# Turning q and k of two batches by a DMA transpose and ScalarE copies in a fused attention and feed-forward kernel

## The chip, the cores and the metric

The kernel runs on one core of a Trainium2 chip. A core has TensorE (PE), which multiplies matrices and can transpose a block by multiplying it with an identity, VectorE (DVE), ScalarE (ACT), GpSimd (POOL) and SyncE (SP), which here only issues transfers. Each engine takes its instructions in the order in which the program gives them to it, and waits on semaphores for what the others produce. Sixteen DMA engines move data; they are fed from queues on SP, ACT and POOL. SBUF is the on-chip memory of 128 partitions. PSUM, where TensorE writes its results, has eight banks, each of 512 fp32 values on every partition.

The metric is the device time in microseconds of one execution of the whole kernel.

## The reference

The inputs q, k and v have the shape (8 batches, 8 heads, 576 tokens, 64). All is fp32.

```
scores = (q @ k^T) / sqrt(64)
heads 0..3: key j is seen by query i if 0 <= i - j < 32          (local)
heads 4..7: key j is seen by query i if j <= i and j % 32 == i % 32   (strided)
x   = softmax(scores) @ v        -> tokens x 512   (4608 x 512, heads side by side)
h   = x @ w_in                   (512 -> 2048)
g   = max(h, 0) + alpha * min(h, 0)
out = g @ w_out                  (2048 -> 512)
```

## The kernel before

**Feed-forward.** The 4608 tokens are cut into nine stages of 512. A stage n has 32 steps. Steps 0 to 15 (`lin1_piece`, L571 to L596) each make one 128 x 512 block of h by four matmuls (L583); ScalarE makes the negative part (L591) and VectorE the result g (L594). Steps 16 to 31 make the output. In stage 1 they are `lin2_piece` (L600 to L628): four matmuls of 512 columns each (L622), and after every fourth step one output tile is copied by ScalarE (L627) and stored by SP (L628). From stage 2 on they are `lin2_fast` (L671 to L734), a scheme with fewer products that works with sums of blocks of g. Those sums (gsum, L652) are made by VectorE and GpSimd at fixed steps, and each pair of `lin2_fast` steps reads one of them.

**Attention.** A pair g is two heads of one batch, 4 pairs to a batch: pairs 4b and 4b + 1 are local, 4b + 2 and 4b + 3 strided. The work of batch n + 1 is done in small pieces between the steps of stage n. A list of pieces is built once (L475 to L545), and `attn_step` (L555) puts the next one out. For a counter g the pieces are in this order: scores of pair g (S, `score_both`), first product with v of pair g - 1 (P), the q transposes of pair g + 1's unit (T), a second P, the k transposes (Tk), and a third P for a strided pair. So batch 3's local q and k are turned while g is 11 and read by the scores of pairs 12 and 13; batch 4's while g is 15, read by those of pairs 16 and 17. These fall into stage 1's and stage 2's second halves. A batch's two local pairs share a pair of tiles, qTs[0] and kTs[0]; index e of them is the pair, and each pair's scores read one e.

**How local q and k get there.** For batches 0 to 4 a transfer (`load_qk`, L97) puts 9 consecutive tokens of the two heads of one pair on each partition, in fp32: partition 2p + e holds tokens 9p to 9p + 8 of pair e. A cast (`cast_l`, L177) makes an fp16 tile [128, 9, 2, 64]: partition, token t within the partition, head within the pair, feature. For batches 2 to 4 GpSimd does it in the list or ScalarE ahead of it. `transpose_piece` (L254) then transposes nine 128 x 128 blocks on TensorE (L269), five into one PSUM bank and four into another. For batch 2 and later ScalarE evicts both (L272 and L273, shown under the line of the helper, L207), and in doing so puts the tokens in order: token 9p + t comes from partition p of block t. Batches 5 to 7 take another way (`load_rows`, `turn_rows`): the load itself casts and lays the rows so that DMA transposes write qTs and kTs directly.

**Order and buffers around it.** `score_both` writes its scores into one two-bank PSUM tile (sp) and into two slots of a ring of three one-bank slots (ps); the products P, the transposes and two other users take slots from the same ring. The exponentials of the second half (L382) are not put out at once but by one per `attn_step` (the list `defer`). SP's queue has, in program order: the DMA transposes of finished attention outputs (`x_dma`, L446 and L443), those of strided q and k (`transpose_d`, L175), and the output stores. In the stretch before batch 3's turn, the casts of batch 3's q and k are in g = 9, pair 8's `x_dma` ends g = 9, and pair 9's comes late in g = 10.

Of the kernel before, what the change touches and what calls it, by code (L numbers as in the profile page):

```python
# [10 lines left out]
F16 = mybir.dt.float16  # L11
# [21 lines left out]
def kernel(  # L33
# [10 lines left out]
    nc = tc.nc  # L44
    keep = tc.keep_in_program_order
# [11 lines left out]
    hpool = ctx.enter_context(tc.tile_pool(name="half", bufs=4))  # L57
# [26 lines left out]
    DX = 2  # L84
    qTs = [cpool.tile([128, 2, 672], F16, name=f"qT{i}") for i in range(2)]
    kTs = [cpool.tile([128, 2, 672], F16, name=f"kT{i}") for i in range(2)]
# [8 lines left out]
    cast16 = {}  # L95
# [12 lines left out]
    NX = 5  # L108
# [13 lines left out]
    def turn_rows(b):  # L122

        for nm in "qk":
            t16 = loaded[(b, False, nm)]
            for e in range(2):
                o = qTs[0][:, e, 0:576] if nm == "q" else kTs[0][:, e, 32:608]
                keep(nc.sync.dma_start_transpose(
                    o.rearrange("r (w p) -> r w p", p=96), t16[0:96, 768 * e : 768 * e + 768]))

    def load_d(b):

        for nm, src in (("q", q), ("k", k)):
            keep(nc.gpsimd.dma_start(
                qks[nm][0:72], src[b, 4:8, :, :].rearrange("h (p t) d -> p h (t d)", t=8)))
# [41 lines left out]
    def cast_l(b, nm, eng="pool"):  # L177
        t16 = hpool.tile([128, 9, 2, 64], F16, tag=f"{nm}l16", bufs=2, name=f"{nm}l16")
        cast_copy(eng, t16, loaded[(b, False, nm)].rearrange("p f (t d) -> p t f d", t=9))
        cast16[(b, False, nm)] = t16  # L180

    def load_v(b, strided):


        if strided:
            st = spool.tile([128, 2048], F16, tag="v", bufs=2, name="stv")
            step = 2 if b == 0 else 4
            for h in range(0, 4, step):
                keep(nc.gpsimd.dma_start(
                    st[0:72, 512 * h : 512 * (h + step)].rearrange("p (h e) -> p h e", h=step),  # L190
                    v[b, 4 + h : 4 + h + step, :, :].rearrange("h (p t) d -> p h (t d)", t=8)))
            loaded[b] = st
        else:
            v16 = vls[b % 2]
            base = v[b, 0:1, 0:1, :]
            r0 = 32 if b < 2 else 0
            step = 12 if b == 0 else 24
            for c in range(0, 24, step):
                keep(nc.gpsimd.dma_start(
                    v16[r0:128, c : c + step, 0:64],  # L200
                    bass.AP(tensor=base.tensor, offset=base.offset + (96 * c - 32 + r0) * D,
                            ap=[[D, 128 - r0], [96 * D, step], [1, D]])))
            cast16[(b, False, "v")] = v16

    def cast_copy(eng, o, i):
        if eng == "act":
            keep(nc.scalar.copy(o, i))  # L207
        elif eng == "dve":
            keep(nc.vector.tensor_copy(o, i))
        else:  # L210
            keep(nc.gpsimd.tensor_copy(o, i))  # L211
# [42 lines left out]
    def transpose_piece(u, nm):  # L254

        b = u // 2  # L260
        early = b < NEARLY
        src = cast16[(b, False, nm)]
        dst = qTs[u % 2][:, :, 0:576] if nm == "q" else kTs[u % 2][:, :, 32:608]
        o = dst.rearrange("r e (p t) -> r e p t", t=9)
        tps = []
        for t0, t1 in ((0, 5), (5, 9)):
            tp = pspool.tile([128, 8, 64, 2], F16, tag="ps", name="tp")
            for t in range(t0, t1):
                keep(nc.tensor.transpose(  # L269
                    tp[:, t - t0].rearrange("r p e -> r (p e)"), src[:, t].rearrange("p f d -> p (f d)"), ident))  # L270
            tps.append(tp[:, 0 : t1 - t0].rearrange("r t p e -> r e p t"))
        cast_copy("act", o[:, :, :, 0:5], tps[0])  # L272
        cast_copy("dve" if early and (u or nm == "k") else "act", o[:, :, :, 5:9], tps[1])  # L273
# [186 lines left out]
    def feed(fn, g):  # L460
        pieces.append((g, fn))

    def T(u, nm):
        return lambda: transpose_piece(u, nm)

    def Sc(g, i):
# [2 lines left out]
    def Pv(g, i):  # L469
        return lambda: pv_piece(pairs[g], i)  # L470

    def X(g, eng=None):
        return lambda: x_piece(pairs[g], eng or ("act" if pairs[g].strided else "dve"))

    for g in range(7, npair + 2):  # L475
        c = g // 4
        a, p, t = g, g - 1, g + 1
        okA = 8 <= a < npair
        okP = 8 <= p < npair
        okT = 8 <= t < npair and t < 4 * NX and (t % 4 == 0 or t < 4 * DX and t % 2 == 0)  # L480
        nP = len(pairs[p].pgroups) if okP else 0
        seq = []
        if okA:
            seq.append(("S", lambda a=a: score_both(pairs[a])))
        if okP:
            seq.append(("P", Pv(p, 0)))
        if okT:
            seq.append(("T", T(t // 2, "q")))
        if 8 <= g - 2 < npair and not pairs[g - 2].xd:
            seq.append(("X", X(g - 2)))  # L490
        if okP:
            seq.append(("P", Pv(p, 1)))
        if okT:
            seq.append(("Tk", T(t // 2, "k")))
        if nP == 3:
            seq.append(("P", Pv(p, 2)))
        if not seq:
            seq.append(("N", lambda: None))

        todo = [(c, pr) for pr in range(2)] if g % 4 == 0 and 8 < g < npair else []  # L500

        if g % 4 == 1 and 9 <= g and c + 1 < B:
            todo = [(c + 1, nm) for nm in "qk"]
        lastP = max([i for i, z in enumerate(seq) if z[0] == "P"], default=len(seq) - 1)
        nslots = [i for i, z in enumerate(seq) if z[0][0] != "S"] or list(range(len(seq)))
        for i, (kind, fn) in enumerate(seq):
            extra = []
            if todo and i in nslots:
                left = len([z for z in nslots if z >= i])
                cnt = -(-len(todo) // max(1, left))  # L510
                extra = [todo.pop(0) for _ in range(min(cnt, len(todo)))]

            def run(fn=fn, extra=extra, g=g, c=c, kind=kind, lastp=(i == lastP), first=(i == 0),
                    second=(i == min(1, len(seq) - 1))):
                fn()
                for b, pr in extra:
                    if pr in ("q", "k"):
                        if b < NX:
                            cast_l(b, pr)
                        if b + 1 < NX:  # L520
                            load_qk(b + 1, pr)
                        continue
                    cast_v(b, pr, "pool")
                    if pr == 1 and b + 1 < B:
                        load_v(b + 1, True)
                if first and g % 4 == 2 and NX <= c + 1 < B:
                    turn_rows(c + 1)
                if lastp and g % 4 == 3 and NX <= c + 2 < B:
                    load_rows(c + 2, "k")
                if lastp:  # L530
                    if 4 * DX <= g - 1 < npair and pairs[g - 1].xd:
                        x_dma(pairs[g - 1])
                    if g % 4 == 3 and DX < c + 1 < B:
                        transpose_d()
                    if g % 4 == 2 and DX <= c and c + 1 < B:
                        load_d(c + 1)
                    if g % 4 == 1 and DX <= c and c + 1 < B:
                        load_v(c + 1, False)
                    if g % 4 == 1 and NX <= c + 2 < B:
                        load_rows(c + 2, "q")  # L540
                    if g == 8:
                        load_v(3, True)
                if second and 4 * DX <= g - 3 < npair and pairs[g - 3].xd and pairs[g - 3].strided:
                    after.append(lambda: x_copy(pairs[g - 3]))
            feed(run, g - 2 if kind == "X" else -1)  # L545

    pos = {"i": 0}
# [2 lines left out]

        return max(i for i, (g, _) in enumerate(pieces) if g == 4 * b + 3) + 1

    late, after = [], []

    def attn_step(end):  # L555
        while late:
            late.pop(0)()
        if pos["i"] < end:
            pieces[pos["i"]][1]()
            pos["i"] += 1  # L560
        if defer:
            defer.pop(0)()
        while after:
            after.pop(0)()

# [181 lines left out]
    def warm(n):  # L747

        for _ in range(n):
# [12 lines left out]
            name=nc.get_next_instruction_name(), act_func_set_id=6, ins=[], outs=[]  # L762
# [29 lines left out]
    def attn_n(n, end):  # L792
        for _ in range(n):
            attn_step(end)
        if n == 0:
            attn_step(0)
# [164 lines left out]
```

## Time and profile before

| | us |
|---|---|
| median of 3 runs | 301.82 (301.68 to 301.95) |
| the profiled execution's own time | 301.52 |
| its span | 299.7 |
| TensorE busy | 293.2 (98%) |
| VectorE busy | 219.1 (73%) |
| ScalarE busy | 178.6 (60%) |
| GpSimd busy | 171.9 (57%) |

All times in the profile are microseconds from the start of the span, unless they are marked ns. A line of a timeline gives the start, the duration, the engine, the line of the kernel, the operation, and what it writes and reads; xN is the number of instructions merged in it, and a bracket at the end is the engine's idle time before it, with what ended that. PE is a matmul, PEld a weight load, and SPq or POOLq the issuing of a transfer. A line of the chain that ended last gives the start, the duration, the engine, what it writes and its line. In groups of instructions the figures after the bar are the busy time in all, the mean of one in ns, and the engine's idle time before them. Matmuls are pipelined, so the busy time of a group of them contains some latency: four matmuls of 512 columns show 1.03, while the next one can follow after 0.86. A helper's operations all stand under the helper's line (L207 for ScalarE copies).

### The profile page before, as it was taken

What the parts mean: (1) busy time and instruction counts of PE and PEld (TensorE: products, weight loads), DVE (VectorE), ACT (ScalarE), POOL (GpSimd) and SP (SyncE); (2) the same over time, 40 slices, a digit from 0 to 9 for tenths busy, and PEclk for the clock granted to TensorE, in tenths of its full rate; (3) what the DMA queues carried; (4) which work ended last, traced back from release to release, by engine and by line L of the source; (5) the groups of instructions that cost most, each with busy time, mean ns of one, the idle gap of its engine ahead of it and who ended that gap; (6) DMA issues with size and microseconds to landing.
All of it is one profiled execution on the core that took longest, in us unless ns stands there. A gap on an engine that the chain in (4) does not pass through costs nothing.

```text
span 299.7 us, 6824 instructions
## 1 busy us (share of the span) xinstructions
PE 293.2 (98%) x2683; PEld 181.8 (61%) x2683; DVE 219.1 (73%) x408; ACT 178.6 (60%) x330; POOL 171.9 (57%) x160
## 2 busy tenths in 40 slices
PE   8999999999999999999999999999999999999995
PEld 3754545554544478646864686468745964684584
DVE  5677886668775897588848984898489948926852
ACT  1676755698457765776477647764676356416730
POOL 8362270049969998979897987595563305002300
PEclk9999999999999999999999999999999999999999
DMA  7999999999996969999989999966811140022004
GB/s 184 257 191 199 241 211 264 198 209 298 115 204 133 113 101 102 177 178 125 132 147 181 139 150 163 208 95 95 193 22 21 24 140 0 2 72 70 0 2 141
DMA packets 96976, 41.18 MB, mean 137 GB/s; under 512 B 75360, under 2 KB 93232, under 8 KB 96944
## 3 DMA queue, kind: packets, MB, share of 16 engines
q0 software_dynamic: 51008, 17.77, 59.0%
q1 hardware_dynamic: 45584, 22.32, 35.1%
q10 hardware_dynamic: 352, 0.66, 0.9%
q8 instruction: 21, 0.34, 0.5%
q14 instruction: 11, 0.09, 0.1%
HBM read 38.24 MB, written 9.44 MB: 159 GB/s over the span
## 4 chain that ended last, share of the span: by engine, by line
PE 84%; DVE 7%; ACT 4%; issue 2%; DMA 2%; SPq 0%; DVEq 0%; ACTq 0%
PE hps L583 37%; PE ops L708 24%; PE ops L622 5%; PE pv L406 4%; PE ops L864 3%; DVE gsum L652 2%; DVE gT L594 2%; PE sp L353 2%; DMA consts<-consts 2%; ACT neg L591 1%; PE xp L429 1%; PE sph L353 1%; DVE x L415 1%; PE ops L879 1%; ACT et L382 1%
## 5 line engine op out<-in xcount | busy, mean ns | idle before, releaser
L583 PE MATMUL hps<-xT,win 128*128 128x512 f16 x576 | 131.9, 379 | 0.2 <-ACT xT L452 0.2
L594 DVE SCALAR_TENSOR_TENSOR gT<-neg,oma,hps 128x512 f16<-128x512 f32 x144 | 105.3, 744 | 36.5 <-ACT neg L591 28.4
L591 ACT ACTIVATE neg<-hps 128x512 f32<-128x512 f32 x144 | 85.8, 598 | 35.7 <-PE hps L583 33.7
L583 PEld LDWEIGHTS <-win 128*128 128x128 f16 x576 | 53.7, 98 | 59.2 <-issue 0.5
L652 POOL TENSOR_TENSOR gsum<-gT 128x1024 f16<-128x1024 f16 x14 | 29.7, 2123 | 42.2 <-DVE gT L594 37.2
L378 POOL TENSOR_TENSOR et<-et,consts 128x576 f16<-128x576 f16 (+1 forms) x24 | 34.7, 1446 | 30.7 <-ACT et L376 30.5
L708 PEld LDWEIGHTS <-gsum 128*128 128x128 f16 x448 | 40.9, 98 | 7.3 <-DVE gsum L652 1.9
L708 PE MATMUL ops<-wsum,gsum 128*128 128x256 f16 x328 | 41.6, 273 | 0.3
L708 PEld LDWEIGHTS <-gT 128*128 128x128 f16 x336 | 31.5, 98 | 5.4 <-issue 0.3
L415 DVE TENSOR_TENSOR x<-pv,rc 96x384 f16<-96x384 f32 (+2 forms) x62 | 33.0, 532 | 2.1
L385 POOL TENSOR_TENSOR et<-et,consts 128x576 f16<-128x576 f16 (+1 forms) x24 | 31.4, 1309 | 0.0
L406 PEld LDWEIGHTS <-et 72*128 72x128 f16 (+1 forms) x448 | 23.4, 98 | 11.4 <-issue 1.8
L708 PE MATMUL ops<-wout,gT 128*128 128x256 f16 x224 | 27.9, 273 | 0.1
L376 ACT ACTIVATE et<-sp 128x576 f16<-128x576 f32 (+1 forms) x24 | 15.5, 644 | 17.1 <-PE sp L353 17.1
L413 DVE RECIPROCAL rc<-pv 96x6 f32<-96x6 f32 (+2 forms) x80 | 14.7, 183 | 10.6 <-PE pv L406 10.4
L211 POOL COPY vs<-stv 72x1024 f16<-72x1024 f16 x12 | 13.3, 1115 | 15.2 <-DMA stv<-in_v_dram 15.2
L663 DVE TENSOR_TENSOR osb<-ops,par 128x512 f32<-128x512 f32 (+1 forms) x14 | 9.4, 673 | 16.1 <-PE ops L708 8.2
L382 ACT ACTIVATE et<-sph 128x288 f16<-128x288 f32 (+1 forms) x48 | 18.8, 409 | 0.0
L661 ACT COPY osb<-ops 128x512 f32<-128x512 f32 x14 | 8.2, 585 | 16.8 <-PE ops L708 16.7
L622 PE MATMUL ops<-wout,gT 128*128 128x512 f16 x64 | 16.4, 379 | 0.0
L406 PE MATMUL pv<-vs,et 72*128 72x65 f16 x256 | 15.4, 193 | 0.8 <-ACT qT L207 0.5
L725 ACT COPY par<-ops 128x512 f32<-128x512 f32 x13 | 7.6, 585 | 14.1 <-PE ops L708 14.1
(105 smaller groups left out, 331.8 us busy)
## 6 DMA issues: line engine op xcount, KB each, us to landing
out_dram<-osb SPq DMA_DIRECT2D x35, 256.0 KB, 4.0
vl<-in_v_dram POOLq DMA_DIRECT2D x6, 384.0 KB, 9.3
win<-in_moe_w_in_dram POOLq DMA_DIRECT2D x4, 512.0 KB, 17.6
wout<-in_moe_w_out_dram POOLq DMA_DIRECT2D x4, 512.0 KB, 15.6
qsd<-in_q_dram POOLq DMA_DIRECT2D x7, 288.0 KB, 6.2
ksd<-in_k_dram POOLq DMA_DIRECT2D x7, 288.0 KB, 7.6
stv<-in_v_dram POOLq DMA_DIRECT2D x7, 288.0 KB, 7.8
ql<-in_q_dram SPq DMA_DIRECT2D x3, 576.0 KB, 7.3
```

Source lines behind the costliest of these rows:

```text
L376: keep(nc.scalar.activation(ev.rearrange("r (y c) -> r y c", y=2), sp[0:r, :, 0:n], AF.Exp, scale=SCALE))
L378: keep(nc.gpsimd.tensor_tensor(mv, mv, m, op=ALU.mult))
L382: keep(nc.scalar.activation(ev[:, n * y : n * y + n], sps[y][0:r, 0:n], AF.Exp, scale=SCALE))
L385: keep(nc.gpsimd.tensor_tensor(mv, mv, m, op=ALU.mult))
L406: keep(nc.tensor.matmul(pv[:, 65 * x : 65 * x + 65], et[0:r, c : c + 128], v16[0:r, 2 * P.pr + hh, t, :] if P.strided else v16[:, 6 * (2 * ...
L415: keep(nc.vector.tensor_tensor(P.x16[0:w, c0 : c0 + 64 * nb].rearrange("r (c e) -> r c e", e=64), pvv[:, :, 0:64], rc[0:w, 0:nb].unsqueeze ...
L583: keep(nc.tensor.matmul(hps, win16[:, kk, 128 * m : 128 * m + 128], xT[:, kk, c0 : c0 + 512], start=(kk == 2), stop=(kk == 1)))
L591: keep(nc.scalar.activation(neg, hps, AF.Relu, scale=-1.0))
L594: keep(nc.vector.scalar_tensor_tensor(gTs[n][:, m, :], neg, oma[:, m : m + 1], hps, op0=ALU.mult, op1=ALU.add))
L622: keep(nc.tensor.matmul(ops, gTs[n][:, kf, 128 * mt : 128 * mt + 128], wout16[:, kf, :], start=(kf == 0), stop=(kf == 15)))
L652: keep((nc.vector if eng == "dve" else nc.gpsimd).tensor_tensor(gsum[i][:, hs], a, b, op=op))
L708: keep(nc.tensor.matmul(o, lhs(y), rhs(y), start=(first and y == 0), stop=(y == 7), skip_group_check=True))
```

## The change

For the local q and k of batches 3 and 4, `transpose_piece` is no longer called. A new function, `turn_cols`, issues for each of q and k one DMA transpose of the whole cast tile, 128 x 1152, into a new fp16 tile [128, 9, 128]: its partition is head and feature, its nine blocks are t, and the 128 columns of a block are p with the pair e inside. It is put out right after the scores of pair 10 (batch 3) and pair 14 (batch 4), on SP. A second new function, `order_cols`, is one ScalarE copy that writes qTs or kTs for one e in token order (token 9p + t from block t), from SBUF. Where the list had T and Tk it now adds two such copies each to a list `lazy`; `attn_step` puts out one of them at a time, when it has no deferred exponential to put out. Batches 0 to 2 and 5 to 7 are as before.

```diff
+    def turn_cols(b):
+
+        for nm in "qk":
+            t16 = hpool.tile([128, 9, 128], F16, tag=f"{nm}x", bufs=1, name=f"{nm}x")
+            keep(nc.sync.dma_start_transpose(t16, cast16[(b, False, nm)].rearrange("p t f d -> p (t f d)")))
+            cast16[(b, False, nm)] = t16
+
+    def order_cols(u, nm, e):
+
+        dst = qTs[u % 2][:, e, 0:576] if nm == "q" else kTs[u % 2][:, e, 32:608]
+        cast_copy("act", dst.rearrange("r (p t) -> r p t", t=9),
+                  cast16[(u // 2, False, nm)].rearrange("r t (p e) -> r e p t", e=2)[:, e])
...
     def T(u, nm):
+        if u // 2 > DX:
+            return lambda: lazy.extend([lambda: order_cols(u, nm, 0), lambda: order_cols(u, nm, 1)])
         return lambda: transpose_piece(u, nm)
...
+                if first and g % 4 == 2 and DX < c + 1 < NX:
+                    turn_cols(c + 1)
                 if first and g % 4 == 2 and NX <= c + 1 < B:
                     turn_rows(c + 1)
...
-    late, after = [], []
+    late, after, lazy = [], [], []
...
         if defer:
             defer.pop(0)()
+        elif lazy:
+            lazy.pop(0)()
         while after:
             after.pop(0)()
```

## The prediction

> **What bounds the kernel now.** I read the page first: the span, the busy shares and the chain that ended last. The profiled execution took 301.52 us, 299.7 of them its span; the median of the three runs is 301.82, so the profile stands 0.3 below it.
>
> ```profile
> PE 293.2 (98%) x2683; PEld 181.8 (61%) x2683; DVE 219.1 (73%) x408; ACT 178.6 (60%) x330; POOL 171.9 (57%) x160
> ...
> PE 84%; DVE 7%; ACT 4%; issue 2%; DMA 2%; SPq 0%; DVEq 0%; ACTq 0%
> ```
>
> TensorE is the bound nearly everywhere, so a transpose taken off it shortens the kernel unless something else ends last there. The order of work is fixed in the program, so I then read the timeline, engine by engine, around the four groups of nine transposes that go. For batch 3, first what POOL and the SP queue do before:
>
> ```profile
> 71.54 1.13 POOL L211 CAST ql<-ql 128x1152 f16<-128x1152 f32 x1
> 72.63 1.13 POOL L211 CAST kl<-kl 128x1152 f16<-128x1152 f32 x1
> ...
> 73.08 2.48 SPq L446 DMA_TRANSPOSE xT<-x  x2
> ```
>
> Then TensorE from the q transposes to the products that take a PSUM slot behind pair 12's scores:
>
> ```profile
> 78.43 1.03 PE L622 MATMUL ops<-wout,gT 128*128 128x512 f16 x4
> 79.30 0.67 PE L269 MATMUL tp<-consts,ql 128*128 128x128 f16 x9
> 79.80 1.03 PE L622 MATMUL ops<-wout,gT 128*128 128x512 f16 x4
> ...
> 84.16 0.30 PE L353 MATMUL sp<-qT,kT 64*128 64x96 f16 x6
> ...
> 86.45 0.35 PE L406 MATMUL pv<-vs,et 72*128 72x65 f16 x6
> ```
>
> And ScalarE over the same stretch:
>
> ```profile
> 78.93 0.41 ACT L382 ACTIVATE et<-sph 72x288 f16<-72x288 f32 x1
> 79.77 1.36 ACT L207 COPY qT<-tp 128x640 f16<-128x640 f16 x2 [0.44 <-PE tp L269]
> 82.19 1.36 ACT L207 COPY kT<-tp 128x640 f16<-128x640 f16 x2 [1.05 <-PE tp L269]
> 83.41 0.60 ACT L627 COPY osb<-ops 128x512 f32<-128x512 f32 x1
> 84.57 0.65 ACT L376 ACTIVATE et<-sp 128x576 f16<-128x576 f32 x1 [0.56 <-PE sp L353]
> 85.11 0.71 ACT L382 ACTIVATE et<-sph 128x288 f16<-128x288 f32 x2
> ```
>
> The first consumer of the turned q and k, the scores of pair 12, starts 4.4 us after the place in the order from which the copies are issued (79.79). The chain in order of time has, where batch 4's transposes stand (108.38 and 111.93):
>
> ```profile
> 109.43 3.41 DVE gsum L652 x3
> ```
>
> There VectorE, not TensorE, ends last. Prices of the new copies come from the groups kept apart by shape:
>
> ```profile
> L452 ACT COPY xT<-xs 128x576 f16<-128x576 f16 x4 | 5.3, 1316 | 0.0
> L207 ACT COPY xT<-xp 128x576 f16<-128x576 f16 x8 | 5.1, 641 | 4.8 <-PE xp L429 4.8
> ```
>
> **The change part by part. Removed from TensorE:** four groups of nine transposes. Four 512-wide matmuls pass in 0.86 us (the chain's step for them), so the stream was free at 78.43 + 0.86 = 79.29 and the next matmul began at 79.80: 0.51 us a group; batch 3's k (81.70 to 82.21) and batch 4's q and k give 0.51 too. In all 4 x 0.51 = 2.04 us, 1.02 per batch. All of batch 3's share is on the path.
>
> Batch 4's share I cost at nothing gained. The second half of gsum[0] is ready at 110.56, and PE already idled 0.36 us for it (weight loads, 110.61). Without the q transposes it arrives 0.51 earlier and waits that much more. The three sums run without a break to 112.84; the first product that reads the last of them came half-way through the group that began at 112.44, about 112.87. Without the k transposes it would want it at 112.36 and waits 0.5. Nothing in that VectorE run depends on the transposes. Ends: 0 and 1.02 gained; I take 0.
>
> **Added on SP:** q's and k's transpose, written into the queue after pair 10's scores, so behind pair 8's two transposes (73.08 to 75.56) and ahead of pair 9's (77.06). The casts end at 72.67 and 73.76, so they do not hold them. Issues of transposes of 80x2048, the nearest in bytes (320 KB against 288 here), took 1.26 to 1.88 us on SP, once 3.34. So q is issued at 75.6, k at about 76.9. Landing, from issue: those of 80x2048 took 5.8, 6.9, 3.9, 5.8, 4.7 and 4.5 us; the four of 96x768 4.6 to 7.4. Pair 9's small ones, issued at 77.06 and 78.29 while batch 3's v was being loaded (from 77 to 78.4 the software queue's packets took 234% of the 16 engines' time), needed 6.1 and about 7. I take 5.8 for q, being between the quiet and the loaded ones: it lands at 81.4 (ends 3.9 and 7.4: 79.5 and 83.0). k at 6.1 to 6.9 lands at 83.0 to 83.8. Behind them on SP stand pair 9's transposes, then the stores of two output tiles, pair 10's transpose (84.46) and batch 3's strided ones. They move about 2 us; pair 9's columns are first read after 91.99, and pair 10's, landed at 84.46 + 2.8, are read by ScalarE at 90.11. That costs nothing; with that cover gone, up to 2 us.
>
> **Moved on ScalarE:** per batch four evictions out (1.36 + 1.36 us), four copies from SBUF in, 576 elements each, reading with a jump of 256 bytes from element to element. L452 does the same with a jump of 160 bytes: 1.316 us. An eviction from PSUM of the same size took 0.641. I take 1.316, because source, step and output order are those of L452; 0.64 stays as the low end. Eight copies are 10.5 us against some 5.5 removed. [...]
>
> One copy is issued per step: q's two after the steps Tq and P, k's first after Tk, then the output copy (L627, 0.60), then k's second. ScalarE works in order, so all wait for q's landing. With q at 81.4: q0 to 82.7, q1 to 84.0, k0 to 85.36 (k has landed). Pair 12 reads only the first half of each tile, so its scores can start at about 85.4; PE, 1.02 early, is there at 83.14. It stalls 2.3. Behind k0: L627 to 85.96, k1 to 87.28, the first exponential (0.65) to 87.93, half of L382 (0.36) to 88.29. That last one frees a PSUM slot of the ring of three that pair 11's second product, at 86.45 before, takes (its first two go to pair 12's scores). So that product comes at 88.39: 88.39 - 86.45 = **+1.94 us**, both stalls and the 1.02 gained counted. Ends: q landing at 79.5 gives k0 83.46 and +0.04; at 83.0 +3.5. Of k, a landing up to 84.0 is hidden behind q's copies; at 84.3 it gives +2.2.
>
> **Batch 4 on ScalarE and SP:** issued after pair 12's transpose (96.88 + 1.2), landing by 99.4 + 7.4 = 106.8 at the latest, before the copies' place at 108.3. Then q0 to 109.6, L722 at its old time, q1 to 111.8, the parity copy 112.13 to 112.7, k0 to 114.0, before pair 16's scores at 114.69; k1 to 115.3 pushes the exponential from 115.33 to 115.9, and the product that needs its slot is at 117.87. Nothing; without that cover 0.6.
>
> **Sum:** 301.5 + 1.9 = 303.4 on the profile's own time, 303.8 from the median; I say **303.5**.
>
> **The rivals.** *The copies are cheap (faster).* The place is the same ScalarE sequence. At 0.64 us, with q at 81.4 and k at 82.4, k0 ends at 83.3; at most 0.2 of the 1.02 is lost: 300.5 to 300.8. The copy's price decides: with q at 81.4 it must be under 0.7 for a gain that can be measured, and at 1.316 even q landing before 79.34 (the end of L382 ahead of it) leaves only 0.1. For it speaks L207's row, against it L452's. 0.20.
>
> *It cancels (within 0.2%, 0.6 us, which is about what a measurement here can tell from no change).* q lands in 3.9 to 4.4 us as in the quiet case at 85.80, or the copies are cheap and k lands late (83.5, k0 84.1): 301.5 to 302.1. [...] The rows show 3.9 us at the least for this size. 0.10.
>
> *The stall is larger.* If pair 12's scores are held until the second half of k is written too, or k's issue is held for 3.34 us as once at 60.13 and k lands later for it, the scores start at 87.4 or k0 ends after 86.6: +3.2 to +4.5, so 304.7 to 306. Against it: each copy names one half only. 0.10.
>
> **How the numbers follow.** Forecast 0.60 (+0.7 to +3.5: 302.2 to 305.0), larger stall 0.10, cancelled 0.10, cheap copies 0.20. Slower 0.70, same 0.10, faster 0.20. The range takes in the upper part of the cheap case and the lower half of the larger stall: 300.7 to 305.3.
>
> **What would show it.** L269's matmuls fall from 90 to 54. Four SP transposes appear near 75.6, 77, 98 and 99.4; the first two land 5 to 7 us later. Eight ScalarE copies of 128x576 from SBUF appear, at about 1.3 us. Before pair 12's scores, near 85, TensorE idles about 2 us for ScalarE's kT, and again some half a microsecond two products later; around 109 to 113 it idles about 1 us more than before, for gsum. If the copies show 0.65, or q lands before 79.5, the forecast is wrong; if batch 4 runs ahead of gsum, its zero is.

## The result and the profile after

The changed kernel takes 311.58 us (median of 6 runs, 309.93 to 312.2) against 301.75 for the kernel before (6 runs, 301.49 to 301.95). The ratio is 1.0319, with a 95% interval of 1.0295 to 1.0343. It is slower by 9.8 us, where 1.9 had been forecast, and outside the range of 300.7 to 305.3.

The busy shares of the page and its chain that ended last, for the changed kernel:

```profile
PE 293.4 (95%) x2647; PEld 181.0 (59%) x2647; DVE 218.3 (71%) x408; ACT 182.1 (59%) x330; POOL 170.4 (55%) x160
...
PE 80%; DVE 6%; DMA 6%; ACT 4%; issue 2%; SPq 0%; DVEq 0%; ACTq 0%
```

TensorE has 36 matmuls fewer and yet is not busy for a shorter time, and 4% of the span moved from its part of the chain to DMA. The chain in order of time and the list of waits say where:

```profile
77.43 13.91 DMA kx<-kl
```

```profile
PE sp L366 <- ACT kT L220: 8.9, 1, 8.9
```

One wait of 8.9 us, at the place that the prediction named: pair 12's scores wait for ScalarE's ordered k, and ScalarE for the DMA transpose. The timeline of the same stretch, with the two transposes, the ScalarE copies and the scores:

```profile
76.07 1.27 SPq L135 DMA_TRANSPOSE qx<-ql  x1
...
77.43 3.98 SPq L135 DMA_TRANSPOSE kx<-kl  x1
...
84.29 2.24 ACT L220 COPY qT<-qx 128x576 f16<-128x576 f16 x2 [4.54 <-DMA qx<-ql]
...
91.36 1.16 ACT L220 COPY kT<-kx 128x576 f16<-128x576 f16 x1 [4.83 <-DMA kx<-kl]
...
92.57 0.42 PE L366 MATMUL sp<-qT,kT 64*128 64x96 f16 x6 [8.93 <-ACT kT L220]
```

And the landings of the two, in us from issue:

```profile
qx<-ql SPq DMA_TRANSPOSE x1, 8.2
...
kx<-kl SPq DMA_TRANSPOSE x1, 13.9
```

After the wait TensorE does not run at its old speed. In the stretches shown next, the columns are the stretch, its length, the busy time of PE, PEld, DVE, ACT and POOL, the granted clock, the DMA share and GB/s:

```profile
88.00:92.00 4.00, 0.00 (x0) 0.00 (x0) 0.00 (x0) 0.64 (x1) 0.00 (x0) 0.50 1.17 157
92.00:94.00 2.00, 1.43 (x15) 0.74 (x16) 0.00 (x0) 2.00 (x4) 0.00 (x0) 0.50 0.10 38
94.00:96.00 2.00, 2.00 (x11) 0.93 (x10) 0.54 (x2) 1.23 (x4) 1.30 (x2) 0.50 0.74 191
96.00:98.00 2.00, 2.00 (x13) 1.01 (x12) 0.77 (x3) 0.00 (x0) 2.00 (x2) 0.71 0.93 162
98.00:100.00 2.00, 2.00 (x25) 0.95 (x23) 1.76 (x4) 1.03 (x2) 1.89 (x3) 1.00 0.95 164
```

The clock fell to half during the wait and came back only near 97. TensorE is "busy" there, but four matmuls of 512 columns (at 93.17) show 1.89 us instead of 1.03.

Setting the two chains beside each other gives the account. The same piece of work starts at these times, before and after:

| piece | before | after | later by | added since the row above |
|---|---|---|---|---|
| first long run of stage 1 | 57.50 | 57.92 | 0.42 | 0.42, ahead of the change |
| pair 12's scores | 84.16 | 92.57 | 8.41 | 7.99 |
| stage 2's first matmuls | 92.15 | 102.72 | 10.57 | 2.16 |
| stage 3's first matmuls | 123.62 | 132.97 | 9.35 | -1.22 |
| end of the span | 299.7 | 309.3 | 9.6 | 0.25 |

The 7.99 are, to 0.1, the wait of 8.93 less the 1.02 saved on transposes. The 2.16 stand where the clock is low. Batch 4's stretch runs 1.22 faster. The last 0.25 come behind TensorE's last matmul, with the last store. The 0.42 lies ahead of everything that was changed; in other runs of the changed kernel's relatives below it was there or not (0.39 in one, 0.00 in another), so it is put down here to the single execution.

### The profile page after: what moved, and what is told of

The parts are those of the page before. It is cut to its first block, busy times and chain, and to the rows that moved or that the text cites. A ratio compares the mean times of both kernels' runs of the same rounds, so it can differ in the third digit from the quotient of the medians.

```text
span 309.3 us, 6759 instructions
## 1 busy us (share of the span) xinstructions
PE 293.4 (95%) x2647; PEld 181.0 (59%) x2647; DVE 218.3 (71%) x408; ACT 182.1 (59%) x330; POOL 170.4 (55%) x160
## 4 chain that ended last, share of the span: by engine, by line
PE 80%; DVE 6%; DMA 6%; ACT 4%; issue 2%; SPq 0%; DVEq 0%; ACTq 0%
PE hps L602 36%; PE ops L727 24%; DMA kx<-kl 4%; PE pv L419 4%; PE ops L641 3%; PE ops L883 3%; DVE gT L613 2%; PE sp L366 2%; DMA consts<-consts 2%; ACT neg L610 1%; PE xp L442 1%; DVE gsum L671 1%; PE sph L366 1%; DVE x L428 1%; PE ops L898 1%
## 5 line engine op out<-in xcount | busy, mean ns | idle before, releaser
L224 POOL COPY vs<-stv 72x1024 f16<-72x1024 f16 x12 | 12.3, 1031 | 17.3 <-DMA stv<-in_v_dram 17.3
L366 PEld LDWEIGHTS <-kT 64*128 64x128 f16 x392 | 8.7, 96 | 19.0 <-ACT kT L220 10.1
L641 PE MATMUL ops<-wout,gT 128*128 128x512 f16 x64 | 17.8, 410 | 0.0
L366 PE MATMUL sp<-qT,kT 64*128 64x72 f16 (+1 forms) x196 | 8.6, 203 | 8.9 <-ACT kT L220 8.9
```

Of the source, the lines that this page charges most:

```text
L366: keep(nc.tensor.matmul(sps[y][:, w * x : w * x + w], P.kT[hf, k0 : k0 + 128], P.qT[hf, q0 : q0 + w], start=(x == 0), stop=(x == len(grp) ...
L641: keep(nc.tensor.matmul(ops, gTs[n][:, kf, 128 * mt : 128 * mt + 128], wout16[:, kf, :], start=(kf == 0), stop=(kf == 15)))
```

## The experiments

The theory after this profile: the transposes are held by loads that are under way on the same 16 DMA engines. In this stretch these are batch 3's local v (issued at 74.1), its strided q and k (78.1 and 78.9), all from POOL's queue, and batch 4's local q and k, ahead of them in SP's own (the last of these landed at 77.5, so it meets only the start of q's). The rival: a transpose of 128x1152 is that slow by itself.

**Two loads moved ahead.**

```diff
-                    if g % 4 == 2 and DX <= c and c + 1 < B:
+                    if g % 4 == 2 and DX < c and c + 1 < B:
                         load_d(c + 1)
-                    if g % 4 == 1 and DX <= c and c + 1 < B:
+                    if g % 4 == 1 and DX < c and c + 1 < B:
                         load_v(c + 1, False)
...
                     if g == 8:
                         load_v(3, True)
+                        load_d(3)
...
     load_qk(3, "k")
+    load_v(3, False)
```

> The changed kernel, but batch 3's local v is loaded ahead of stage 1's list and batch 3's strided q and k two pieces earlier, so that neither load is under way when batch 3's transposes run. Theory (the software queue's loads hold up the transposes): q lands within 6 us and k within 7 us of issue instead of 8.2 and 13.9, TensorE's wait before pair 12's scores falls from 8.9 us to under 2, the clock stays at full speed, and the time is 299.5 to 303. Rival (a 128x1152 transpose is that slow by itself, or is held by pair 8's transposes ahead of it on SP): k still lands 12 us or more after issue and the time stays above 309.

Measured: 308.21 us, ratio 1.0217 (1.0202 to 1.0233). The wait fell only to 5.6 us; q landed after 9.8 us and k after 9.3. Neither expectation was met. The move had not emptied the stretch: the strided loads, now issued at 68.4 and 69.1, needed 14.7 and 16.3 us, so they were in flight until 85.4.

**The same move in the kernel before.** The same edit as above, on the kernel before.

> The kernel before with the same two loads moved and nothing else, so that the move's own worth is known. Both theories: within 1 us of the kernel before (301 to 302.7), since nothing on TensorE waits for these loads.

Measured: 301.74 against 301.71, ratio 1.0002 (0.9992 to 1.0011). The move is worth nothing by itself, so what the other runs gain by it, they gain through the transposes.

**Batch 4 alone.**

```diff
-        if u // 2 > DX:
+        if u // 2 > DX + 1:
...
-                if first and g % 4 == 2 and DX < c + 1 < NX:
+                if first and g % 4 == 2 and DX + 1 < c + 1 < NX:
                     turn_cols(c + 1)
```

> The change for batch 4 alone; batch 3 is turned on TensorE as before. If the gain read from the changed kernel's trace for batch 4 (1.2 us between stage 2's first half and stage 3) is real: 300.3 to 300.9. If batch 4 is worth nothing, as predicted: 301.4 to 302.0.

Measured: 301.98, ratio 1.0009 (1.0000 to 1.0018): no gain, as predicted. TensorE saves its 1.02 us of transposes and waits 0.78 us for VectorE's sums in their place, as this trace's timeline of the two shows:

```profile
109.81 1.14 DVE L671 TENSOR_TENSOR gsum<-gT 128x1024 f16<-128x1024 f16 x1
...
111.01 1.48 PE L727 MATMUL ops<-wsum,gsum 128*128 128x256 f16 x12 [0.58 <-DVE gsum L671]
...
112.69 1.21 PE L727 MATMUL ops<-wsum,gsum 128*128 128x256 f16 x8 [0.20 <-DVE gsum L671]
```

**TensorE kept busy in the wait.** 38 matmuls of 512 columns, whose result is not used, stand on TensorE in front of pair 12's scores. In the chain of the changed kernel eight such matmuls pass in 1.73 us, so 38 are an estimated 8.2 us of work for the wait of 8.9.

```diff
                 sps = [sp[:, y] for y in range(2)]
+                for _ in range(38 if P.g == 12 else 0):
+                    keep(nc.tensor.matmul(sps[0], wrm[:, 0:128], wrm, start=True, stop=True))
             grp = P.sgroups[i]
```

> [...] If the lowered clock after the wait costs about 2.1 us of its own: the clock stays at 1.00 and the time falls to 309 to 310. If that loss is the queue of late scores and exponentials and not the clock: 311 to 312.

Measured: 310.65, ratio 1.0301 (1.0286 to 1.0316). The clock did as the first expectation said, the time did not. k landed after 13.8 us, as before, and TensorE had 0.68 us left to wait. Its timeline, and the stretch in which the scores start:

```profile
83.06 8.37 PE L358 MATMUL sp<-wrm 128*128 128x512 f16 x38
92.10 0.30 PE L368 MATMUL sp<-qT,kT 64*128 64x96 f16 x6 [0.68 <-ACT kT L220]
```

```profile
90.00:94.00 4.00, 3.32 (x32) 1.57 (x31) 0.25 (x2) 3.12 (x4) 0.00 (x0) 1.00 0.36 112
```

The clock stayed at full speed, and stage 2 began at 100.21, 8.06 later than before, where the changed kernel had 10.57 - 0.42 = 10.15. So the lowered clock cost 2.1 us. Only 0.9 of that shows at the end; stage 2's sums were slower here (last section).

**Three loads out of the way.** Batch 3's v and strided loads as in the first run, and batch 4's local q and k behind pair 9's transposes:

```diff
-                        if b + 1 < NX:
+                        if b + 1 < NX and b != 3:
                             load_qk(b + 1, pr)
...
                         x_dma(pairs[g - 1])
+                    if g == 10:
+                        load_qk(4, "q")
+                        load_qk(4, "k")
```

> As the run with batch 3's v and strided loads moved ahead, and batch 4's local q and k loads (1.15 MB on SP's own queue) put behind pair 9's transposes as well, so that far less is in flight when batch 3's q and k are turned. Theory (what holds the two transposes is the sum of the loads on the 16 DMA engines, on either queue): q and k land within 6 us of issue, TensorE's wait before pair 12's scores is under 2.5 us, 301.5 to 303.5 in all. Rival (transposes of this size take 8 to 14 us whatever else is under way): the wait stays above 5 us and the time above 307.

Measured: 304.95, ratio 1.0127 (1.0092 to 1.0161). With batch 4's loads gone from this stretch the strided loads were further on: the packets of their queue took 24% of the 16 engines' time from 77.2 to 78.2, where in the first run they took 77% from 76 to 84. q landed after 6.7 us and k after 6.2, and the wait was 2.5 us:

```profile
82.70 2.28 ACT L220 COPY qT<-qx 128x576 f16<-128x576 f16 x2 [3.01 <-DMA qx<-ql]
...
84.88 1.15 ACT L220 COPY kT<-kx 128x576 f16<-128x576 f16 x1
...
86.09 0.30 PE L366 MATMUL sp<-qT,kT 64*128 64x96 f16 x6 [2.52 <-ACT kT L220]
```

This is the sequence of the prediction: q's two copies as soon as q is there, k's first behind them, then the scores. The clock stayed at 1.00. The time is above the 301.5 to 303.5 expected; 2.5 - 1.02 = 1.5 us are the wait. By stage 3 the kernel is 2.3 us late, counted from the same lateness at stage 1's start. The chain shows where more was lost: pair 10's transpose, which now stands behind batch 4's loads on SP, landed after 6.1 us instead of 2.8, and stage 2's first matmuls waited for the ScalarE copies behind it:

```profile
86.98 6.14 DMA xs<-x16s
93.14 1.12 ACT xT L465 x2
```

About 1.0 us more comes behind TensorE's last matmul; no run explains that last part.

**Unread transposes in the tail.** Three pairs, issued where loads and transposes were meant to meet:

```diff
+            if (n, i) in ((7, 16), (8, 2)):
+                (load_d(7) if n == 7 else load_v(7, False))
+            if (n, i) in ((7, 4), (7, 18), (8, 4)):
+                turn_extra()     # for each of q, k: a DMA transpose of batch 4's cast tile into a new tile
```

> The kernel before, which also turns batch 4's cast tiles into a tile that nobody reads, three times in the tail, where few loads are left: alone (stage 7, step 4), right after loads of strided q and k (1 KB packets, stage 7, step 18), and right after a load of local v (small packets, stage 8, step 4). Theory: alone q and k land in 3.5 to 5 us; next to either load 2 us or more later. Rival (slow by themselves): 8 us or more in all three.

They did not meet: SP ran ahead to 244.9 to 274, while POOL issued the loads from 254.7 to 257.6. So all six transposes ran with no load beside them. The landings of k's tile (q's are the same):

```profile
DMA to landing us min/median/max: 3.2/3.3/3.3
```

A 128x1152 transpose lands in 3.2 to 3.3 us when no load is under way, a little under the 3.5 to 5 expected. The rival is out. The kernel took 301.78 us against 301.64 before.

**The transposes without a reader.** They are issued as in the changed kernel, but both batches are still turned on TensorE.

```diff
     def turn_cols(b):
...
-            cast16[(b, False, nm)] = t16
...
-        if u // 2 > DX:
+        if u // 2 > B:
```

> The changed kernel's four DMA transposes are issued at their places, but batches 3 and 4 are still turned on TensorE and evicted by ScalarE as before, and nobody reads the DMA's result. Theory (the loss is the wait for the landing, not the extra load on the DMA engines): within 0.6 us of the kernel before, though k still lands 10 us or more after issue. Rival (the extra transfers delay other transfers that the kernel waits for): 304 or more.

Measured: 307.7, ratio 1.0207 (1.0156 to 1.0258), against an expectation of no change; the rival's 304 or more is met. With nobody waiting for q and k, the kernel still loses 6 us. Its waits, the landing of pair 10's transpose, and the ScalarE copy that reads it:

```profile
PE hps L601 <- ACT xT L464: 4.0, 2, 3.8
```

```profile
xs<-x16s SPq DMA_TRANSPOSE x1, 9.4
```

```profile
94.90 1.40 ACT L464 COPY xT<-xs 128x384 f16<-128x384 f16 x2 [4.71 <-DMA xs<-x16s]
```

Pair 10's transpose stands behind k's and pair 9's in SP's queue. It landed 2.8 us after issue in the kernel before and 9.4 here; stage 2's first matmuls waited 3.8 us for it, and the clock was at 0.50 until about 101. So the extra transfers hurt by what they hold up as well as by their own lateness. Whether they do so by their load or by standing ahead in the same queue, no run separates. In the changed kernel this second damage is not seen: pair 10's transpose was issued only at 93.45, landed after 2.7 us and was read at 100.68.

**Half of the change.** Batch 3's k alone by DMA, the three loads moved:

```diff
-        for nm in "qk":
+        for nm in "k":
...
-        if u // 2 > DX:
+        if u // 2 == DX + 1 and nm == "k":
```

> Batch 3's k alone is turned by DMA and put into order by ScalarE, its q and all of batch 4 stay on TensorE; the three loads are moved as in the first run of this call. If one transpose lands within 6 us of its issue at 76: no wait, 0.5 us gained, 301.0 to 301.5. If it lands 9 us or more after issue: pair 12's scores wait 2 to 4 us, 304 to 306.

Measured: 302.96, ratio 1.0050 (1.0033 to 1.0066). k landed in 5.7 us and TensorE did not wait for it. The landing was met and the time was not. TensorE's chain ends at 296.56, where that of before ends at 296.54, so the 0.5 us are given back by then. The chain shows the place: as in the run with three loads out of the way, pair 10's transpose stands behind batch 4's moved loads, lands late, and stage 2's start hangs on it:

```profile
84.00 6.52 DMA xs<-x16s
```

The span is 1.2 us longer after TensorE's end, 0.4 in the last sum and 0.8 in the last store. From the last sum's end to the span's end it takes 3.5 us here, 2.7 in the kernel before, and 2.6 to 3.3 in seven other traces. No run tells why.

**v moved alone, strided q and k put off alone.** The first is one half of the first experiment's edit, on `load_v`. The second:

```diff
-                    if g % 4 == 2 and DX <= c and c + 1 < B:
+                    if g % 4 == 2 and DX < c and c + 1 < B:
                         load_d(c + 1)
...
+                    if g == 11:
+                        load_d(3)
                     if g % 4 == 3 and DX < c + 1 < B:
                         transpose_d()
```

> The changed kernel with batch 3's local v alone loaded ahead of stage 1's list; the strided q and k loads stay where they were. If v's small packets are what holds batch 3's q: q lands 2 us or more sooner than 8.2 us after issue, and k, then still next to the strided loads, at 10 us or more; 306 to 309. If v is not the one: no change, 310 to 312.

> The changed kernel with batch 3's strided q and k loads alone put off by one pair, behind the place where batch 3's k was turned. If these loads are what holds k: q lands as before (about 8 us after issue), k by 9 us instead of 13.9, TensorE's wait before pair 12's scores falls from 8.9 to 3 to 5 us, 303.5 to 306.5. If v and the loads on SP's own queue hold it: k still 12 us or more, 309 to 312.

Measured for v: 308.67, ratio 1.0232 (1.0192 to 1.0272); q landed after 7.1 us (8.2 before the move), k after 10.1. q came 1.1 us sooner, not 2, and k 3.8 us sooner; but the strided loads were issued earlier here too (76.5 instead of 78.1), so not all of that need be v's. For the strided loads, issued at 81.3 instead of 78.1: 306.06, ratio 1.0142 (1.0127 to 1.0158), as the first expectation had it; q landed after 8.1 us as before, and k:

```profile
kx<-kl SPq DMA_TRANSPOSE x1, 7.6
```

```profile
PE sp L366 <- ACT kT L220: 3.8, 1, 3.8
```

So putting off the strided loads alone took 6.3 us off k's 13.9, the most of the single moves tried.

One more transfer stood ahead of q in the same queue: pair 8's second transpose. In the changed kernel it was issued at 74.8 and landed after 6.3 us, at about 81.0, and q landed 3.2 us behind it. In three other runs q came 2.4 us (two loads moved), 3.5 (v alone) and 3.4 (strided loads put off) behind it. No run took pair 8's transposes away, so how much of q's 8.2 us is this place in the queue, and how much the loads, is not shown.

**The meeting in the tail, held back.** The transposes were made to wait for a small VectorE write to their source:

```diff
+            if (n, i) in ((7, 9), (8, 9)):
+                (load_d(7) if n == 7 else load_v(7, False))
+            if (n, i) in ((7, 14), (8, 14)):
+                turn_extra()     # now with a one-column write to the cast tile ahead of each transpose
```

> As the run with three unread pairs of transposes in the tail, where each landed in 3.2 to 3.3 us with nothing else under way, but now each pair is held back until a load runs beside it: the strided q and k (stage 7) and a local v (stage 8). Theory: q or k lands at 5 us or more in both. Rival (two loads and the rest of stage 1's traffic are needed together): within 0.5 us of 3.3.

Beside the strided loads q landed after 5.6 us and k after 5.3. The pair meant to meet v was issued at 285.1, four us behind it; up to 286.0 only v's queue had moved packets, and it landed in 3.5 and 3.4. So the strided loads alone, with nothing else going on, add 2 us; the second half says nothing of v. The kernel took 302.33, ratio 1.0018 (1.0007 to 1.0029), which is of no interest here.

## Why the prediction was wrong

**The step that failed is the landing of the two transposes, k's above all.** It was taken as 5.8 us for q, with 7.4 as the far end, and 6.1 to 6.9 for k, from the rows of other transposes; k, at 83.0 to 83.8, was to be hidden behind q's copies. Measured were 8.2 for q, which makes 84.3, and 13.9 for k, which makes 91.3, so that k ended the wait. In the run with the strided loads put off, q landed after 8.1 us, k was hidden again, and the wait was 3.8 us. So q's lateness is worth about 3.8 of the 8.9 us, where 2.3 had been forecast, and k's the other 5.1.

The rows had been measured with the loads that were then around them. With no load under way the transpose needs 3.3 us, less than any row it was taken from; beside the strided loads 5.3 to 5.6; here 8.2 and 13.9. A landing is thus no property of the transfer alone. Pair 8's transposes, ahead in the queue, were counted by their issue (to 75.56); in the kernel before the second of them landed only at about 79.5 (5.2 us after its issue). The profile before had shown the loads (the software queue at 234% of the engines' time) and pair 9's small transposes at 6 to 7 us instead of 2.4. This was used to pick a value within the rows, where it should have widened the far end: the new transposes carry several times the bytes of pair 9's through the same stretch, and lie in front of them.

**The clock was no term of the sum.** A wait of 8.9 us brought it to half, and that cost 2.1 us more, shown by filling the wait. A wait of 2.5 us left it at 1.00 (three loads out of the way). Of the two waits of 3.8 us, the one in the run without a reader was followed by 0.50 (96 to 100), and behind the one with the strided loads put off four matmuls of 512 columns showed 1.89 us instead of 1.03. Behind those of 5.1, 5.6 and 8.9 us pair 12's first scores took 0.42 us, where they took 0.30 behind the wait of 2.5. The moment differs: the clock fell 3.3 us after TensorE's last matmul in the changed kernel (it is 0.87 in the mean of 84 to 88), but about 2.0 us after it in the run without a reader (0.77 in the mean of 92 to 96), and about 4.1 in the one with the strided loads put off, when the scores had begun (0.30 us for the first six at 87.23, 0.37 for the next). The far end of q's landing gave a stall of nearly 4 us in the prediction; but TensorE's longest wait in the profile before is 1.2 us, so that profile could not show what one of 4 us costs.

**"That costs nothing", of what stands behind on SP.** Wrong, with the cover named rightly (pair 10's transpose, read at 90.11) and its price without cover set at 2 us. The run without a reader showed 3.8 us of waiting at that place, the low clock again, and 6 us in all. In the changed kernel itself the later stage 2 kept the cover.

**The place was right, and the order where k was not late.** The stall is where it was put. In the changed kernel it ended with k's landing and one copy. With three loads out of the way, the landing of 6.7 us gave the scores at 86.09, one copy after another as worked out.

**The copies:** 1.316 us was taken, 1.19 measured (the mean of eight), so L452 was the right row and L207's 0.64 was not. Why this read takes nearly twice as long as an eviction of the same size is not shown: no run here varied the step alone.

**The second stall,** 0.65 us for a PSUM slot, was not seen. In the run with 6.7 us of landing the next scores come 4.5 us after the first, against 4.4 before.

**Batch 4 at nothing** was right for the change in itself (1.0009 alone, with the two waits for gsum). It rested on VectorE's sums ending last there. In the changed kernel they ended sooner, and the stretch came out 1.2 us faster (last section).

**The rivals.** "Cheap copies" falls by their price. "It cancels" falls by the 8.2 and 13.9. "The stall is larger" had the right sign and too small a size, because it let k be late by one slow issue only.

## What to carry to other kernels

When work moves from an engine to the DMA queues, price its landing from what is in flight, and ahead of it in its queue, at that place and time, and not from such transfers elsewhere: here the same transfer took 3.3 us with no load beside it and 13.9 us between loads and behind another. Then look at what stands behind it in its queue, because that can get later too even if nobody reads the new transfer (here 9.4 us from issue instead of 2.8). A stall of the bounding engine can have a second price: here waits of 3.8 us and more were followed by a halved clock, one of 2.5 was not, and after the 8.9 it cost 2.1 us.

## What the runs showed that had not been expected

VectorE's three sums of stage 2 took 1.9 us in some runs and 3.4 or 4.2 in others, and in the slower ones GpSimd's masks ran beside them. In the kernel before, GpSimd's masks (L378 and L385, 108.73 to 111.63) run beside them; in the changed kernel the masks were over at 120.0 and GpSimd issued loads:

```profile
109.43 1.13 DVE L652 TENSOR_TENSOR gsum<-gT 128x1024 f16<-128x1024 f16 x1
110.48 2.36 DVE L652 TENSOR_TENSOR gsum<-gsum,gT 128x1024 f16<-128x1024 f16 x2
```

```profile
120.00 0.69 DVE L671 TENSOR_TENSOR gsum<-gT 128x1024 f16<-128x1024 f16 x1
120.60 1.29 DVE L671 TENSOR_TENSOR gsum<-gsum,gT 128x1024 f16<-128x1024 f16 x2
```

That is 3.4 us for three sums beside the masks and 1.9 without, and these sums are on the chain. The run without a reader shows a third case, sums clear of the masks while batch 4 is still turned on TensorE:

```profile
116.04 0.69 DVE L670 TENSOR_TENSOR gsum<-gT 128x1024 f16<-128x1024 f16 x1
116.65 1.29 DVE L670 TENSOR_TENSOR gsum<-gsum,gT 128x1024 f16<-128x1024 f16 x2
```

From the last twelve matmuls of L583 that the chain shows in stage 2 to stage 3's first ones it takes, in us and in single executions:

| run | batch 4 turned on TensorE | the three sums | stretch |
|---|---|---|---|
| before | yes | 3.4 | 21.81 |
| batch 4 alone | no | 3.4 | 21.57 |
| without a reader | yes | 1.9 | 21.27 |
| the change | no | 1.9 | 20.59 |

So of the 1.22 us, 0.54 come with the faster sums alone, and the other 0.68 come with the transposes taken off TensorE. While the sums run beside the masks, taking them off is worth only 0.24. In the run with the filled wait, masks of 1.7 us each ran beside all three sums and they took 4.2 us, which fits that only part of the clock's 2.1 us was seen at the end. Why a sum takes longer beside a mask is not shown, and that moving the masks would give this gain to the kernel before was not tried.
